# The last batch's inverse transform inside the feed-forward: eight units on four 64x64 tiles in place of sixteen pieces on the full array

## The chip, the cores and the metric

One core of a Trainium2 chip runs the kernel. Its engines are TensorE (PE, with its weight loads as PEld), VectorE (DVE), ScalarE (ACT), GpSimd (POOL) and SyncE (SP), which here issues nearly all DMAs. The metric is device time in microseconds (us) of one execution, as the median of several; less is better.

## The reference

```python
X = np.fft.rfft(x, axis=1)                 # x: 8 batches, 3008 positions, 256 channels
Yr = Xr @ w_r - Xi @ w_i + b_r             # complex linear layer on every frequency
Yi = Xr @ w_i + Xi @ w_r + b_i
Y = softshrink(Yr, 0.01) + 1j * softshrink(Yi, 0.01)
y = np.fft.irfft(Y, n=3008, axis=1)        # 8 x 3008 = 24064 rows of 256
g = y @ w_gate                             # 256 -> 1536
out = (g * sigmoid(g) * (y @ w_val)) @ w_out   # 1536 -> 256
```

## The kernel before

The kernel has two phases. `transform` makes the Fourier transform, the complex layer, the shrink and the inverse transform batch by batch; `gated_ffn` makes the gated feed-forward over 24 blocks of rows. They overlap little: the feed-forward begins at about 520 us and runs to the end.

The second half of the inverse transform (47 positions n for each of 64 residues) is a set of small products. For a residue m and its partner m+32 (index g = 0 or 1) it multiplies, over 48 rows (24 frequencies, real and imaginary), z (48 x 256 channels) with a constant table (48 x 47). For batches 0 to 6 this is done in `transform` by `unit` (lines 616 to 666): a unit takes four m, and as the two g lie at partitions 0 and 64 and the 256 channels are cut in four groups of 64, every matmul uses one 64x64 quarter of the array, 48 rows by 64 columns, with 47 columns moving. It is 4 m x 2 halves of the channels x 2 g x 2 sides = 32 matmuls (line 638), into two PSUM banks, one for each g. ACT copies both banks into an SBUF tile `xt` (line 650, 128x376 each), and a DMA writes it to `xt_d`.

The last batch's rows are needed only by the blocks from 20 on, so its share is done inside the feed-forward by `inverse` (lines 1012 to 1025): 16 pieces of two m, each piece four matmuls of 96 rows (both g in the rows, `co` being a table with zeros between) by 128 columns with 94 columns moving, into the bank `b1`. fp32 matmuls show as two records each, so a piece is 8 records and a unit is 64. ACT copies the bank (line 1024, 128x376), and a DMA writes it out.

In the feed-forward a block has 6 steps q, each with a gate half (n = 0) and a value half (n = 1), made by `gate_or_value` (line 902). Its operations are written out by hand in issue order for PE, DVE, ACT and POOL (`manual_schedule`, line 1052); SP's order is made by the framework. A half makes seven products `up` of three matmuls each (line 780, 128x128 weights, 512 columns; the last two blocks have 384) and, between them, the `down` products of the pair before, of three matmuls each. The matrices are multiplied by a scheme with seven products instead of eight, so sums of inputs and outputs are taken on DVE and POOL. The banks are `b1`, `b2`, `b3`, `spare` and four totals: all eight of PSUM.

The order on PE in the gate half is up 1, up 5, down 1, up 6, down 3, up 2, up 7, up 3, down 2, up 4; the next half begins with up 1 into `b1` and up 5 into `b2`. Where a piece is due (q = 2 of blocks 1 to 16) it stands between up 7 and up 3. `b1` is then free as soon as `take(H11, b1)` has read it, an ACT Silu (line 925) that waits for up 2. After up 3, ACT makes the Silu of H22 (its input is in SBUF) and then of H12 (from `b2`), a cast for T4 (line 796), and after up 4 the Silu of H21. ACT then copies `b1` to `b3` at the start of the next half (line 932).

`load_z` fetches a piece's z and its table (lines 1009, 1010); it is queued in the block before the piece's q = 2. The up weights `wup` come over a ring of four tiles, each loaded three halves ahead (line 215), on the same SP queue.

Of the kernel before, what the change touches and what calls it, by code (L numbers as in the profile page):

```python
# [9 lines left out]
F32 = mybir.dt.float32  # L10
# [7 lines left out]
P = 128  # L18
B = 8
SEQ = 3008  # L20
C = 256
FF = 1536
N1 = 47
N2 = 64
NM = 32
NK = 24
# [3 lines left out]
UM = 4  # L30
NU = NM // UM
UT = UM * 2 * N1
# [33 lines left out]
def fourier_constants():  # L66
    n = float(SEQ)
    k1 = np.arange(NK)
    n1 = np.arange(N1)
    n2 = np.arange(N2)  # L70
    k2 = np.arange(N2)

    def turn(num, den):
        a = 2.0 * np.pi * (np.asarray(num) % den) / den
        c, s = np.cos(a), np.sin(a)
        c[np.abs(c) < 1e-14] = 0.0
        s[np.abs(s) < 1e-14] = 0.0
        return c, s

    c, s = turn(np.outer(n1, k1), N1)  # L80
    wa = np.zeros((2, 64, 2, 32))
    wa[:, :N1, 0, :NK] = c
    wa[:, :N1, 1, :NK] = -s
    wa = wa.reshape(P, 64)

    k = k1[:, None] + N1 * k2[None, :]
    c, s = turn(n2[None, :, None] * k[:, None, :], SEQ)
    re = np.concatenate([c, s], 1)
    im = np.concatenate([-s, c], 1)
    lo = np.arange(N2) < 32  # L90
    wf = np.concatenate([np.where(lo, re, im), np.where(lo, im, re)], 2)
    wf = wf.reshape(NK, 2, 2, 32, P).transpose(2, 1, 3, 0, 4).reshape(P, NK, P)

    c, s = turn(np.outer(k2, n2), N2)
    yr = np.concatenate([c, s], 1)
    yi = np.concatenate([-s, c], 1)
    w = np.where(k2 < 32, 2.0, np.where(k2 == 32, 1.0, 0.0))
    w[0] = 1.0
    wi = []
    for scale in (w, np.full(N2, 2.0)):  # L100
        a, b = yr * scale[:, None], yi * scale[:, None]
        if scale is w:
            b[0] = 0.0
            b[32] = 0.0
        wi.append(np.concatenate([np.where(lo[:, None], a, b), np.where(lo[:, None], b, a)], 0))
    wi = np.stack(wi, 1)

    m = np.arange(NM)
    wo = np.zeros((2, 2, NK, NM, 2, N1))
    for gg in range(2):  # L110
        num = k1[:, None, None] * (64 * n1[None, None, :] + 32 * gg + m[None, :, None])
        c, s = turn(num, SEQ)
        wo[0, gg, :, :, gg] = c / n
        wo[1, gg, 1:, :, gg] = -s[1:] / n
    wq = np.zeros((2, 64, NM * N1))
    for gg in range(2):
        wq[gg, : 2 * NK] = wo[:, gg, :, :, gg].transpose(1, 0, 2, 3).reshape(2 * NK, NM * N1)
    wq = wq.reshape(P, NM * N1)
    wo = wo.reshape(4, NK, NM * 94).transpose(1, 0, 2).reshape(96, NM * 94)
    f = lambda a: np.ascontiguousarray(a, np.float32)  # L120
    return {"wa": f(wa), "wf": f(wf), "wi": f(wi), "wo": f(wo), "wq": f(wq)}


def f32(ap):
# [123 lines left out]


@with_exitstack  # L250
def spectral_ffn(ctx: ExitStack, tc: tile.TileContext, xp, w_r, w_i, cb, wup_raw, wdn_raw, ca, cf, ci, co, cq, out):
    nc = tc.nc
    const = ctx.enter_context(tc.tile_pool(name="const", bufs=1))
    dram = ctx.enter_context(tc.tile_pool(name="dram", bufs=2, space=DRAM))
    w21 = const.tile([P, 2, P], F32R, name="w21")
    ring = ctx.enter_context(tc.tile_pool(name="ring", bufs=RING, reuse_waits="tile"))
    xt_d = [dram.tile([P, 2, SEQ], F32, name=f"xt_d{b}", bufs=1) for b in range(B)]
    d2 = {B - 1: dram.tile([NK, P, C], F32, name="d2_last", bufs=1)}
    wup_d = [dram.tile([P, 2, 7 * P], F32, name=f"wup_d{u}", bufs=1) for u in range(2 * NQ)]
    wdn_d = [dram.tile([P, 2, 7 * P], F32, name=f"wdn_d{q}", bufs=1) for q in range(NQ)]  # L260


    front = ctx.enter_context(tc.tile_pool(name="front", bufs=1))
    ps_ = ctx.enter_context(tc.tile_pool(name="ps", bufs=1, space=PSUM))
    feed = Feed(nc, front, ring, wup_d, xt_d)

    with ExitStack() as tail:
        last = tail.enter_context(tc.tile_pool(name="last", bufs=2, side="right"))
        with ExitStack() as one:
            finish = transform(one, tc, front, ring, last, ps_, feed, xp, w_r, w_i, cb, wup_raw, wdn_raw, ca, cf, ci, cq, w21, wup_d, wdn_d, xt_d, d2)  # L270
        finish()
        ffn = gated_ffn(ctx, tc, front, ring, ps_, feed, co, w21, wdn_d, xt_d, d2[B - 1], out)
        next(ffn)
    next(ffn, None)

# [480 lines left out]
    return finish  # L756


def gated_ffn(ctx, tc, front, ring, ps_, feed, co, w21, wdn_d, xt_d, d2, out):

    nc = tc.nc
    v, g, act = nc.vector, nc.gpsimd, nc.scalar
# [10 lines left out]
    b1, b2, b3, spare = [room(tag) for tag in ("ps_a", "ps_b", "mixb0", "ps_s")]  # L773
# [3 lines left out]
    def product(o, weights, parts, start, stop):  # L777

        for i, (w, x) in enumerate(((1, 0), (0, 0), (0, 1))):
            nc.tensor.matmul(o, lhsT=weights[w], rhs=parts[x], start=start and i == 0, stop=stop and i == 2, skip_group_check=True)  # L780


    H11, H12, H22, H21, T1, T3, T2, T4 = range(8)
    RIGHT = {1: H11, 3: H22, 2: H21, 5: T1, 7: T3, 4: T4, 6: T2}

    def at(i, h):
        return hidden[:, i, :h] if i < 4 else more[:, i - 4, :h]

    def diff(pair, o, a, b):
        h = pair["h"]  # L790
        v.tensor_tensor(at(o, h), at(a, h), at(b, h), op=ALU.subtract)  # L791

    def upper(pair, i):
        h = pair["h"]
        pair[i] = sbr.tile([P, 2, T], F32R, name="h_parts", bufs=8)
        act.copy(pair[i][:, 0, :h], at(i, h))  # L796
# [5 lines left out]
    def down(pair, n_):  # L802

        h, q = pair["h"], pair["q"]
        weights = [wdn[q][:, x, A_AT[n_], :] for x in range(2)]
        parts = [pair[RIGHT[n_]][:, x, :h] for x in range(2)]
        if n_ in total:
            product(total[n_][:, :h], weights, parts, q == 0, q == NQ - 1)
        else:
            product(spare[:, :h], weights, parts, n_ == 1, True)  # L810
# [4 lines left out]
    def add(pair, n_):  # L815
        h = pair["h"]
        o = sums[:, SUM_AT[n_], :h]
        if pair["q"] == 0:
            v.tensor_copy(o, spare[:, :h])
        else:  # L820
            v.tensor_tensor(o, o, spare[:, :h], op=ALU.add)  # L821
# [80 lines left out]
    def gate_or_value(pair, last, n, k, extra):  # L902

        blk, q, h = pair["blk"], pair["q"], pair["h"]
# [17 lines left out]
        def take(i, src):  # L922

            if n == 0:
                act.activation(at(i, h), src, AF.Silu)  # L925
            else:
                v.tensor_tensor(at(i, h), at(i, h), src, op=ALU.mult)  # L927

        gate = n == 0 and last
# [45 lines left out]
        last_sum = b1[:, :h] if n else m5  # L975
        v.tensor_tensor(last_sum, m5, b3[:, :h], op=ALU.add)  # L976
        if gate:
            diff(last, T4, H21, T2)
            add(last, 1)
            if q == 2 and blk in pieces:  # L980
                inverse(pieces[blk])
        up(b2, 3, False)
        take(H22, last_sum)
        take(H12, b2[:, :h])
        if n:
            upper(pair, H22)
            lower(g, pair, H22)
        if gate:
            upper(last, T4)
            lower(g, last, T4)  # L990
            if first:
                step("after d7")
            down(last, 2)
            if closing:
                ends["now"] = result(last)
                step("after d2")
# [3 lines left out]
        take(H21, b3[:, :h])  # L1000


    pieces = {i + 1: i for i in range(NM // 2)}
    part = {}

    def load_z(u):
        z = part["z"] = sbr.tile([96, 2 * C], F32, name="z2")
        w = part["w"] = sbr.tile([96, 2 * 94 + 160], F32, name="w2")[:, : 2 * 94]
        nc.sync.dma_start(z, d2.rearrange("k (q m) c -> (k q) (m c)", m=NM)[:, u * 2 * C : (u + 1) * 2 * C])
        nc.sync.dma_start(w, co[:, u * 188 : (u + 1) * 188])  # L1010

    def inverse(u):
        for cc in range(2):
            for i in range(2):
                nc.tensor.matmul(  # L1015
                    b1[:, cc * 188 + i * 94 : cc * 188 + (i + 1) * 94],
                    lhsT=part["z"][:, i * C + cc * P : i * C + (cc + 1) * P],
                    rhs=part["w"][:, i * 94 : (i + 1) * 94],
                    start=cc == 0 and i == 0,
                    stop=True,  # L1020
                    skip_group_check=True,
                )
        xt = sbr.tile([P, 2, 188], F32, name="xt2")
        act.copy(xt.rearrange("p a b -> p (a b)"), b1[:, :376])
        nc.sync.dma_start(xt_d[B - 1][:, :, u * 188 : (u + 1) * 188], xt)


    todo = {}

# [19 lines left out]
    sbr = ctx.enter_context(tc.tile_pool(name="sb3", bufs=1, side="right", reuse_waits="tile"))  # L1049
    last = None  # L1050
    k = 0
# [57 lines left out]
```

## Time and profile before

| | us |
|---|---|
| median of 3 runs | 2579.42 (2577.97 to 2581.5) |
| the profiled execution | 2577.29 |
| its span, first to last instruction | 2575.3 |
| busy in the span: PE / PEld | 2556.2 / 2141.6 |
| busy: DVE / ACT / POOL | 2060.2 / 1706.7 / 2072.8 |
| granted TensorE clock, mean | 1.000 |

The profiled execution has 2.0 us outside its span. Matmuls overlap each other in the records: a product of three is shown as 0.84 us long, but products follow each other start to start in 0.68 us, and it is starts that are compared below.

### The profile page before, as it was taken

To read this page: it belongs to the slowest core of one execution; us is meant where nothing else is said; L and a number is where in the kernel's file an instruction comes from. 1 tells how busy PE (TensorE), PEld (TensorE's weight loads), DVE (VectorE), ACT (ScalarE), POOL (GpSimd) and SP (SyncE) were. 2 spreads that over 40 slices of the span, in tenths; PEclk is the share of its full clock that TensorE was granted. 3 is DMA by queue.
4 is the path that set the end of the run, shared out by engine and by line. 5 is a ranking of instruction groups with operands and counts; after the bars stand their busy time and mean duration, and the time that the engine had idled before them with its cause. 6 is when DMAs were issued, how large, how long until landed. Compare 5 with 4: busy or idle time off the path is not lost.

```text
span 2575.3 us, 45125 instructions
## 1 busy us (share of the span) xinstructions
PE 2556.2 (99%) x16168; PEld 2141.6 (83%) x16168; DVE 2060.2 (80%) x3001; ACT 1706.7 (66%) x3345; POOL 2072.8 (80%) x1588
## 2 busy tenths in 40 slices
PE   9999999999999999999999999999999999999999
PEld 6788888988888888888888888888888888888899
DVE  7888888668778877877788787878877887888787
ACT  5788888866656666666656666665666666666665
POOL 4777777568888888888888888888888888888886
PEclk9999999999999999999999999999999999999999
DMA  6688888855445444544444455444444444444453
GB/s 231 217 281 275 280 280 264 279 204 190 150 145 167 161 153 153 168 149 146 163 164 151 147 169 168 150 147 159 167 149 144 161 162 149 141 162 158 147 186 122
DMA packets 137360, 460.89 MB, mean 179 GB/s; under 512 B 13872, under 2 KB 61616, under 8 KB 137136
## 3 DMA queue, kind: packets, MB, share of 16 engines
q1 hardware_dynamic: 137136, 458.01, 53.5%
q8 instruction: 128, 2.10, 0.3%
q14 instruction: 96, 0.79, 0.1%
HBM read 366.99 MB, written 90.96 MB: 178 GB/s over the span
## 4 chain that ended last, share of the span: by engine, by line
PE 91%; ACT 4%; DVE 3%; issue 1%; POOL 1%; DMA 1%; ACTq 0%; SPq 0%; POOLq 0%; DVEq 0%
PE bank L780 78%; PE mixb L528 3%; PE ps_b L506 2%; PE ps_s L513 2%; PE ps_z L552 2%; PE ps_a L469 1%; PE ps_x L638 1%; ACT t L540 1%; PE bank L1015 1%; DVE d L474 1%; ACT f_hi L563 0%; ACT z L586 0%; DVE f_lo L566 0%; POOL t L574 0%; DVE f L565 0%
## 5 line engine op out<-in xcount | busy, mean ns | idle before, releaser
L780 PE MATMUL bank<-x_near,wup 128*128 128x512 f32 (+1 forms) x4032 | 1037.5, 386 | 0.3 <-DVE bank L954 0.2
L800 POOL TENSOR_TENSOR h_parts<-more,h_parts 128x512 fp32r<-128x512 f32 (+1 forms) x572 | 847.4, 1494 | 110.5 <-ACT h_parts L796 96.7
L780 PEld LDWEIGHTS bank<-x_near,wup 128*128 128x128 f32 x4032 | 750.6, 188 | 150.9 <-DVE bank L954 3.6
L780 PE MATMUL bank<-h_parts,wdn 128*128 128x512 f32 (+1 forms) x3021 | 835.8, 385 | 0.4 <-DVE h_parts L800 0.4
L800 POOL TENSOR_TENSOR h_parts<-hidden,h_parts 128x512 fp32r<-128x512 f32 (+1 forms) x431 | 563.8, 1319 | 205.4 <-ACT h_parts L796 162.7
L780 PEld LDWEIGHTS bank<-h_parts,wdn 128*128 128x128 f32 x3021 | 564.7, 188 | 109.3 <-DVE h_parts L800 0.7
L796 ACT CAST h_parts<-hidden 128x512 fp32r<-128x512 f32 (+1 forms) x433 | 265.6, 614 | 450.3 <-DVE hidden L927 449.1
L780 PE MATMUL bank<-x_parts,wup 128*128 128x512 f32 (+1 forms) x2016 | 526.5, 384 | 0.0
L927 DVE TENSOR_TENSOR hidden<-hidden,bank 128x512 f32<-128x512 f32 (+1 forms) x576 | 376.0, 674 | 77.9 <-PE bank L780 69.6
L821 DVE TENSOR_TENSOR sums<-sums,bank 128x512 f32<-128x512 f32 (+1 forms) x357 | 240.3, 673 | 243.5 <-PE bank L780 243.4
L780 PEld LDWEIGHTS bank<-x_parts,wup 128*128 128x128 f32 x2016 | 375.2, 188 | 71.3 <-DVE bank L954 1.7
L796 ACT CAST h_parts<-more 128x512 fp32r<-128x512 f32 (+1 forms) x572 | 349.3, 611 | 39.1 <-DVE more L791 28.6
L925 ACT ACTIVATE hidden<-bank 128x512 f32<-128x512 f32 (+1 forms) x432 | 252.6, 585 | 114.7 <-PE bank L780 114.3
L791 DVE TENSOR_TENSOR more<-hidden 128x512 f32<-128x512 f32 (+1 forms) x286 | 291.8, 1059 | 0.0
L791 DVE TENSOR_TENSOR more<-hidden,more 128x512 f32<-128x512 f32 (+1 forms) x286 | 257.6, 901 | 0.0
L932 ACT COPY bank<-bank 128x512 f32<-128x512 f32 (+1 forms) x288 | 161.6, 561 | 109.9 <-DVE hidden L927 103.9
L954 DVE TENSOR_TENSOR bank<-hidden,bank 128x512 f32<-128x512 f32 (+1 forms) x288 | 197.0, 684 | 35.7 <-PE bank L780 23.3
L574 POOL TENSOR_TENSOR t<-t,y 128x512 f32<-128x512 f32 x96 | 132.6, 1382 | 90.3 <-DVE y L573 86.6
L940 ACT COPY hidden<-bank 128x512 f32<-128x512 f32 (+1 forms) x288 | 167.6, 582 | 2.5
L540 ACT COPY t<-mixb 64x256 f32<-64x256 f32 x384 | 140.9, 367 | 21.1 <-PE mixb L528 13.6
L244 POOL TENSOR_TENSOR x_near<-xf,x_near 128x512 fp32r<-128x512 f32 (+1 forms) x112 | 142.1, 1285 | 5.3 <-PE bank L780 4.7
L976 DVE TENSOR_TENSOR hidden<-hidden,bank 128x512 f32<-128x512 f32 (+1 forms) x144 | 97.4, 676 | 43.4 <-PE bank L780 43.2
(107 smaller groups left out, 3105.9 us busy)
## 6 DMA issues: line engine op xcount, KB each, us to landing
wup<-wup_d SPq DMA_DIRECT2D x288, 896.0 KB, 4.6
scratch<-xp SPq DMA_DIRECT2D x59, 512.0 KB, 5.2
out<-o SPq DMA_DIRECT2D x88, 256.0 KB, 6.1
d<-z SPq DMA_DIRECT2D x84, 256.0 KB, 3.9
z_in<-d SPq DMA_DIRECT2D x112, 192.0 KB, 5.0
xt_d<-xt SPq DMA_DIRECT2D x56, 376.0 KB, 5.2
xf<-xt_d SPq DMA_DIRECT2D x15, 1024.0 KB, 6.9
wup_d<-wup SPq DMA_DIRECT2D x12, 896.0 KB, 5.1
```

What stands on the lines that cost most here:

```text
L244: low = lambda: eng.tensor_tensor(part[:, 1, :h], src, f32(part[:, 0, :h]), op=ALU.subtract)
L540: nc.scalar.copy(t()[64 * half : 64 * half + 64, k * C : (k + 1) * C], mixb[64 * k : 64 * k + 64, half * C : (half + 1) * C])
L780: nc.tensor.matmul(o, lhsT=weights[w], rhs=parts[x], start=start and i == 0, stop=stop and i == 2, skip_group_check=True)
L791: v.tensor_tensor(at(o, h), at(a, h), at(b, h), op=ALU.subtract)
L796: act.copy(pair[i][:, 0, :h], at(i, h))
L800: eng.tensor_tensor(pair[i][:, 1, :h], at(i, h), f32(pair[i][:, 0, :h]), op=ALU.subtract)
L821: v.tensor_tensor(o, o, spare[:, :h], op=ALU.add)
L925: act.activation(at(i, h), src, AF.Silu)
L927: v.tensor_tensor(at(i, h), at(i, h), src, op=ALU.mult)
L932: act.copy(b3[:, :h], b1[:, :h])
L940: act.copy(m5, b2[:, :h])
L954: v.tensor_tensor(b2[:, :h], m5, b3[:, :h], op=ALU.add)
```

## The change

The last batch's inverse is made in 8 units of four m, in blocks 1 to 8, in the form that `unit` has: 32 matmuls on four 64x64 tiles, into `b1` for g = 0 and `b2` for g = 1. As `b2` is in use until the Silu of H12 has read it, the unit is issued later, between down 2 and up 4, and in these halves ACT takes H12 ahead of H22. ACT copies `b1` and then `b2` into the z tile itself (its matmuls are done by then), and one DMA of 376 KB writes it out. z is loaded by two DMAs of 192 KB, the table by one from `cq`, which `transform` uses too; the array `co` is gone.

```diff
         if gate:
             diff(last, T4, H21, T2)
             add(last, 1)
-            if q == 2 and blk in pieces:
-                inverse(pieces[blk])
         up(b2, 3, False)
-        take(H22, last_sum)
-        take(H12, b2[:, :h])
+        between = gate and q == 2 and blk in pieces
+        for one in ((H12, b2[:, :h]), (H22, last_sum))[:: 1 if between else -1]:
+            take(*one)
...
             down(last, 2)
+            if between:
+                inverse(pieces[blk])
...
-    pieces = {i + 1: i for i in range(NM // 2)}
+    pieces = {i + 1: i for i in range(NU)}
...
     def load_z(u):
-        z = part["z"] = sbr.tile([96, 2 * C], F32, name="z2")
-        w = part["w"] = sbr.tile([96, 2 * 94 + 160], F32, name="w2")[:, : 2 * 94]
...
+        z = part["z"] = sbr.tile([P, UM * C], F32, name="z2")
+        w = part["w"] = sbr.tile([P, UM * N1], F32, name="w2")
+        rows = d2.rearrange("k (i g m) c -> g (k i) (m c)", i=2, g=2)
+        for g in range(2):
+            nc.sync.dma_start(z[64 * g : 64 * g + 2 * NK], rows[g, :, u * UM * C : (u + 1) * UM * C])
+        nc.sync.dma_start(w, cq[:, u * UM * N1 : (u + 1) * UM * N1])
 
     def inverse(u):
-        for cc in range(2):
-            for i in range(2):
-                nc.tensor.matmul(
-                    b1[:, cc * 188 + i * 94 : cc * 188 + (i + 1) * 94],
...
-        xt = sbr.tile([P, 2, 188], F32, name="xt2")
-        act.copy(xt.rearrange("p a b -> p (a b)"), b1[:, :376])
-        nc.sync.dma_start(xt_d[B - 1][:, :, u * 188 : (u + 1) * 188], xt)
+        for i in range(UM):
+            for cc in range(2):
+                for g, bank in enumerate((b1, b2)):
+                    rows = slice(64 * g, 64 * g + 2 * NK)
+                    for side in range(2):
+                        col = i * C + cc * P + 64 * side
+                        nc.tensor.matmul(
+                            bank[64 * side : 64 * side + 64, (cc * UM + i) * N1 : (cc * UM + i + 1) * N1],
+                            lhsT=part["z"][rows, col : col + 64],
+                            rhs=part["w"][rows, i * N1 : (i + 1) * N1],
...
+        xt = part["z"][:, : 2 * UT].rearrange("p (c t) -> p c t", c=2)
+        to = xt.rearrange("p c (m g n) -> p c m g n", m=UM, g=2)
+        for g, bank in enumerate((b1, b2)):
+            act.copy(to[:, :, :, g], bank[:, : 2 * UM * N1].rearrange("p (c m n) -> p c m n", c=2, m=UM))
+        nc.sync.dma_start(xt_d[B - 1][:, :, u * UT : (u + 1) * UT], xt)
```

## Rows read from the trace of the kernel before

**Rows 1.** The page: busy time of the engines with their share of the span, and the chain of work that ended last, by engine.
```profile
PE 2556.2 (99%) x16168; PEld 2141.6 (83%) x16168; DVE 2060.2 (80%) x3001; ACT 1706.7 (66%) x3345; POOL 2072.8 (80%) x1588
...
PE 91%; ACT 4%; DVE 3%; issue 1%; POOL 1%; DMA 1%; ACTq 0%; SPq 0%; POOLq 0%; DVEq 0%
```

**Rows 2.** The chain that ended last, within 2000 to 2100 us (start us, us, what).
```profile
1999.80 100.39 PE bank L780 x442
```

**Rows 3.** Busy time by stretch: block 16, the last with a piece, block 17, the first without, and block 9, with a piece. The stretch begins and ends at the block's first copy of line 932; columns: us, then PE, PEld, DVE, ACT, POOL busy with counts, granted clock, DMA share, GB/s.
```profile
1917.20:2004.24 87.04, 86.97 (x388) 71.68 (x387) 69.12 (x96) 54.52 (x98) 73.52 (x54) 1.00 0.46 154
2004.24:2090.02 85.78, 85.78 (x380) 70.89 (x379) 69.16 (x96) 53.96 (x97) 73.53 (x54) 1.00 0.46 154
1307.85:1394.88 87.03, 86.96 (x388) 71.70 (x387) 69.22 (x96) 54.59 (x99) 73.56 (x54) 1.00 0.47 157
```

**Rows 4.** The timeline of PE, and one row of PEld, around the piece in block 16: up 2, up 7, the piece, up 3, down 2, up 4 (start us, us, what, count, and in brackets the idle time before and what ended it).
```profile
1948.30 0.84 PE L780 MATMUL bank<-x_near,wup 128*128 128x512 f32 x3
1948.97 0.84 PE L780 MATMUL bank<-x_parts,wup 128*128 128x512 f32 x3
1949.88 1.13 PE L1015 MATMUL bank<-w,z 96*128 96x94 f32 x8
1950.80 0.93 PE L780 MATMUL bank<-x_parts,wup 128*128 128x512 f32 x3
1951.57 0.86 PE L780 MATMUL bank<-h_parts,wdn 128*128 128x512 f32 x3
1952.26 0.85 PE L780 MATMUL bank<-x_parts,wup 128*128 128x512 f32 x3
...
1949.88 0.97 PEld L1015 LDWEIGHTS bank<-w,z 96*128 96x128 f32 x8 [0.49 <-ACT hidden L925]
```

**Rows 5.** The timeline of ACT in the same place: the Silu of H11, the cast for T2, the piece's copy.
```profile
1949.23 0.60 ACT L925 ACTIVATE hidden<-bank 128x512 f32<-128x512 f32 x1 [0.82 <-PE bank L780]
1949.73 0.61 ACT L796 CAST h_parts<-more 128x512 fp32r<-128x512 f32 x1
1951.05 0.47 ACT L1024 COPY xt<-bank 128x376 f32<-128x376 f32 x1 [0.71 <-PE bank L1015]
```

**Rows 6.** The timeline of PE in the same half of block 17, which has no piece: in the first row the last two matmuls of up 2, then up 7 and up 3 (its third matmul is the last of the eight), then down 2, up 4, up 1 of the next half, up 5.
```profile
2035.55 1.98 PE L780 MATMUL bank<-x_near,wup 128*128 128x512 f32 x8
2037.37 0.84 PE L780 MATMUL bank<-h_parts,wdn 128*128 128x512 f32 x3
2038.05 0.84 PE L780 MATMUL bank<-x_near,wup 128*128 128x512 f32 x3
2038.73 0.84 PE L780 MATMUL bank<-x_parts,wup 128*128 128x512 f32 x3
2039.41 0.84 PE L780 MATMUL bank<-x_near,wup 128*128 128x512 f32 x3
```

**Rows 7.** The timeline of ACT in that half: the cast for T2, Silu of H22, Silu of H12, the cast for T4, Silu of H21, the copy of `b1` to `b3`; and DVE's difference that feeds T4.
```profile
2036.76 0.61 ACT L796 CAST h_parts<-more 128x512 fp32r<-128x512 f32 x1
2037.67 0.63 ACT L925 ACTIVATE hidden<-hidden 128x512 f32<-128x512 f32 x1 [0.29 <-POOL h_parts L800]
2038.21 0.58 ACT L925 ACTIVATE hidden<-bank 128x512 f32<-128x512 f32 x1
2038.69 0.61 ACT L796 CAST h_parts<-more 128x512 fp32r<-128x512 f32 x1
2039.19 0.60 ACT L925 ACTIVATE hidden<-bank 128x512 f32<-128x512 f32 x1
2039.83 0.57 ACT L932 COPY bank<-bank 128x512 f32<-128x512 f32 x1
...
2037.49 0.73 DVE L791 TENSOR_TENSOR more<-hidden,more 128x512 f32<-128x512 f32 x1
```

**Rows 8.** The timeline of PE around a unit of `transform` that stands between full-array work: before it 128x256 matmuls, after it 128x512 ones.
```profile
497.13 0.28 PE L513 MATMUL ps_s<-wm_hi,f_lo 128*128 128x256 f32 x1
497.25 0.28 PE L513 MATMUL ps_s<-wm_lo,f_hi 128*128 128x256 f32 x1
497.46 1.15 PE L638 MATMUL ps_x<-wo,z_in 48*64 48x47 f32 x64
498.54 0.50 PE L552 MATMUL ps_z<-y_hi,wi_hi 128*128 128x512 f32 x1
498.88 0.40 PE L552 MATMUL ps_z<-y_lo,wi_hi 128*128 128x512 f32 x1
499.11 0.39 PE L552 MATMUL ps_z<-y_hi,wi_lo 128*128 128x512 f32 x1
```

**Rows 9.** By line: the unit's matmuls and the ACT copy behind a unit, all of them (duration ns min/median/max, first and last start us).
```profile
L638 PE MATMUL ps_x<-wo,z_in x3584: 202/231/253, 108.8 to 521.8; 48*64 48x47 f32 x200
...
L650 ACT COPY xt<-ps_x x112: 469/481/519, 110.0 to 523.4; 128x376 f32<-128x376 f32 x112
```

**Rows 10.** SP's queue around the piece in block 1 (the next piece's loads, this piece's store, the up weights before and behind), and DMA issues by line (KB each, median us to landing).
```profile
639.40 0.33 SPq L215 DMA_DIRECT2D wup<-wup_d  x1
645.36 0.33 SPq L1009 DMA_DIRECT2D z<-d_last  x1
645.75 0.42 SPq L1010 DMA_DIRECT2D w<-co  x1
646.25 0.57 SPq L1025 DMA_DIRECT2D xt_d<-xt  x1
647.46 14.60 SPq L215 DMA_DIRECT2D wup<-wup_d  x3
...
wup<-wup_d SPq DMA_DIRECT2D x288, 896.0 KB, 4.6
...
xt_d<-xt SPq DMA_DIRECT2D x56, 376.0 KB, 5.2
...
xt_d<-xt SPq DMA_DIRECT2D x16, 188.0 KB, 2.7
```

More of the change, by code (lines that the diff above doesn't have):

```diff
@@ L118, in fourier_constants @@
     wq = wq.reshape(P, NM * N1)
-    wo = wo.reshape(4, NK, NM * 94).transpose(1, 0, 2).reshape(96, NM * 94)
     f = lambda a: np.ascontiguousarray(a, np.float32)
-    return {"wa": f(wa), "wf": f(wf), "wi": f(wi), "wo": f(wo), "wq": f(wq)}
+    return {"wa": f(wa), "wf": f(wf), "wi": f(wi), "wq": f(wq)}
 def f32(ap):
@@ L250, in spectral_ffn @@
 @with_exitstack
-def spectral_ffn(ctx: ExitStack, tc: tile.TileContext, xp, w_r, w_i, cb, wup_raw, wdn_raw, ca, cf, ci, co, cq, out):
+def spectral_ffn(ctx: ExitStack, tc: tile.TileContext, xp, w_r, w_i, cb, wup_raw, wdn_raw, ca, cf, ci, cq, out):
     nc = tc.nc
@@ L271, in spectral_ffn @@
         finish()
-        ffn = gated_ffn(ctx, tc, front, ring, ps_, feed, co, w21, wdn_d, xt_d, d2[B - 1], out)
+        ffn = gated_ffn(ctx, tc, front, ring, ps_, feed, cq, w21, wdn_d, xt_d, d2[B - 1], out)
         next(ffn)
@@ L756, in transform, with gated_ffn @@
     return finish
-def gated_ffn(ctx, tc, front, ring, ps_, feed, co, w21, wdn_d, xt_d, d2, out):
+def gated_ffn(ctx, tc, front, ring, ps_, feed, cq, w21, wdn_d, xt_d, d2, out):
     nc = tc.nc
@@ L1000, in gate_or_value @@
         take(H21, b3[:, :h])
-    pieces = {i + 1: i for i in range(NM // 2)}
+    pieces = {i + 1: i for i in range(NU)}
     part = {}
     def load_z(u):
-        z = part["z"] = sbr.tile([96, 2 * C], F32, name="z2")
-        w = part["w"] = sbr.tile([96, 2 * 94 + 160], F32, name="w2")[:, : 2 * 94]
-        nc.sync.dma_start(z, d2.rearrange("k (q m) c -> (k q) (m c)", m=NM)[:, u * 2 * C : (u + 1) * 2 * C])
-        nc.sync.dma_start(w, co[:, u * 188 : (u + 1) * 188])
-    def inverse(u):
-        for cc in range(2):
-            for i in range(2):
-                nc.tensor.matmul(
-                    b1[:, cc * 188 + i * 94 : cc * 188 + (i + 1) * 94],
[L1017 to L1022, printed above, removed]
-        xt = sbr.tile([P, 2, 188], F32, name="xt2")
-        act.copy(xt.rearrange("p a b -> p (a b)"), b1[:, :376])
-        nc.sync.dma_start(xt_d[B - 1][:, :, u * 188 : (u + 1) * 188], xt)
+        z = part["z"] = sbr.tile([P, UM * C], F32, name="z2")
[4 more added lines that the diff above has]
+        nc.sync.dma_start(w, cq[:, u * UM * N1 : (u + 1) * UM * N1])
@@ new lines, in inverse @@
+    def inverse(u):
+        for i in range(UM):
[8 more added lines that the diff above has]
+                            rhs=part["w"][rows, i * N1 : (i + 1) * N1],
+                            start=True,
+                            stop=True,
+                            skip_group_check=True,
+                        )
+        xt = part["z"][:, : 2 * UT].rearrange("p (c t) -> p c t", c=2)
[3 more added lines that the diff above has]
+        nc.sync.dma_start(xt_d[B - 1][:, :, u * UT : (u + 1) * UT], xt)
@@ L1092 @@
         "ci": k["wi"],
-        "co": k["wo"],
         "cq": k["wq"],
```

## The prediction

> **What bounds the kernel now.** I read the page first, then the chain within one stretch, then the busy time by block, and only then the timeline around one piece. On the page PE is busy for 2556.2 of 2575.3 us, and it is 91% of the chain that ended last [rows 1]. Within the feed-forward the chain has nothing but PE: 100 us without a break by line 780 [rows 2]. So whatever PE is spared there shortens the kernel one for one, and whatever makes PE wait lengthens it; the other engines have 20 to 34% of the span free [rows 1]. The blocks by themselves give the price of a piece: 87.04 and 87.03 us with one, 85.78 without, with PE busy to the last tenth and the granted clock at 1.00 in all three [rows 3]. A piece costs 1.25 us, and sixteen of them 16 x 1.25 = 20.0 us.
>
> The timeline shows what those 1.25 us are [rows 4]. Products follow each other by 0.68 us; from up 7 to the piece it is 0.91, so 0.23 are a wait; the piece lasts 0.92 to the start of up 3; up 3 is followed after 0.77 in place of 0.68, as its weights come in late, which is 0.09; down 2 has 0.01 more. The sum is 1.25. The wait is for ACT's Silu of H11, which must read `b1`: up 2 ends at 1949.14, the Silu begins 0.09 later and lasts 0.60, and PE goes on 0.05 behind its end, though up 7 had only covered until 1949.65 [rows 4, 5].
>
> **The change part by part.** *Removed:* sixteen pieces, 20.0 us. Half of that needs no further argument: blocks 9 to 16 become like block 17, which gives 8 x 1.25 = 10.0 us.
>
> *Added: eight units.* The same 32 matmuls on the same four tiles are in the trace, as `unit` [rows 8, 9]. From the unit's first record to the next full-array matmul it is 498.54 - 497.46 = 1.08 us. Going in, the first tile matmul begins 0.21 after the last 256-column one in place of 0.12: 0.09. Going out, the second product matmul begins 0.34 after the first in place of 0.23: 0.11. A unit that waits for nothing so costs 1.08 + 0.09 + 0.11 = 1.28 us.
>
> It has to wait for the Silu of H12, which reads `b2`, and the cover is again one product of three. Up 3 ends at 2037.53 (2035.55 + 1.98) and the place behind down 2 is at 2038.05 [rows 6]. With H12 first, ACT is free for it (the cast for T2 ends at 2037.37), so it begins at 2037.62, takes 0.58 to 0.60 and lets PE go 0.05 later, at 2038.25 to 2038.27 [rows 5, 7]. That is 0.20 to 0.22 behind the place; the wait takes the place of the 0.09 of going in, since in both cases the weights of the first tile matmul are loaded only then. I take 0.22 + 1.08 + 0.11, and 0.01 for the echo in the next product as behind a piece: 1.42 us. The bounds of one unit are 1.28 (no wait) and, from below, those of the first rival, 2.3.
>
> A rule of the Trainium skill speaks against this. The traced unit has 64 records in 1.15 us, the last of them 0.23 long, so its starts lie 0.92 / 63 = 15 ns apart [rows 8, 9]. The page "TensorE: Matmul & The Clock Gate", section "Wait — 56ns, not 53.3ns?", says that matmul starts never come closer than some 25 ns however few columns there are; an estimate by it makes the unit's starts 63 x 25 ns = 1.58 us long, so 0.66 us more than the row, 5.3 us over eight units. By that the time would be 2576 us. The trace doesn't agree, and its rows are of the very shape that is added.
>
> *ACT's part.* Two copies for each unit by 0.48 us [rows 9] stand for two pieces' copies by 0.47 [rows 5]: no more work, but the copy of `b1` must be done before up 1 of the next half. Count from U, the unit's first matmul (2038.27). The unit ends at U + 1.15. ACT by then has made H12 (to U - 0.05), H22 and the cast for T4, which in the plain half follow each other by 0.5 us each [rows 7], so to about U + 1.0; the difference that the cast reads is done at 2038.22. The piece's copy began 0.04 behind its last matmul (1949.88 + 1.13 to 1951.05) [rows 4, 5], a Silu 0.09 behind [rows 5]. So `b1` is read by U + 1.67 to U + 1.72, and PE may go 0.05 later. PE wants it at U + 1.08 + 0.68 + 0.11 = U + 1.87, behind up 4. It is hidden, by 0.1 to 0.15 us. Without that cover PE would pay each tenth eight times, 0.8 us. The copy of `b2` ends by U + 2.2 and is wanted 0.68 later than `b1`: nothing. Behind the copies on ACT stands the Silu of H21, for which up 4 ends at U + 2.03; in the plain half it too starts 0.3 behind its product's end, and the copy to `b3` behind it is wanted only three products later [rows 6, 7]. Swapping H12 and H22 costs nothing else: both are multiplied in the next half.
>
> *DMAs and SP's queue.* Per unit two z loads, a table load and a store stand for four loads and two stores of two pieces. All of it is on SP, none on PE's path unless the up weights behind it come late. The new wait is this: the z tile is also what the store reads, so the next z load must wait until the store has landed, 2.7 us for 188 KB here and 5.2 for 376 KB in the transform, which bound it [rows 10]. SP was already held by such a load, up to 5.9 us in block 1 (639.40 to 645.36), and the next up weights went at 647.46 all the same, because they waited for PE to free a ring tile [rows 10]. With the store issued at about U + 2.3, the hold ends at U + 5.5 to U + 8, near the time when the next up weights are due (7.1 us behind the one before: 14.60 less 0.33, over two [rows 10]). They are needed three halves later and land in 4.6 us; I take nothing.
>
> *The sum.* 20.0 - 8 x 1.42 = 20.0 - 11.4 = 8.6 us. The profiled execution was 2577.29, so it would be 2568.7. The median shown is 2579.42, 2.1 above; what is compared later is such a median, so I predict 2579.4 - 8.6 = **2570.8 us**. Between the bounds of the waits (0.09 going in; a copy late by 0.1 and the next product with it) the saving is 7.8 to 9.8 us.
>
> **The rivals.**
> First, *ACT holds the unit or the next half longer*. If PE's wait is for H22 as well, it is 0.54 us more (2038.21 - 2037.67 [rows 7]), 4.3 us in all: 2575.1. If up 1 waits for both copies, 2.2 + 0.05 - 1.87 = 0.38 more, 3.0 in all: 2573.8. Both together make a unit cost 2.3 us and leave 1.3 us: 2578.1. For it: ACT runs its queue in order and PE sees it through one count. Against it: PE began the piece 0.05 behind the Silu that it needed, while the cast queued behind that was still running (1949.73 to 1950.34) [rows 4, 5].
>
> Second, *PE issues the unit's records further apart than in the transform*. Each ns more between starts costs 63 ns a unit and 0.5 us in all; from 7 ns more on, 22 in place of 15, the saving falls under 5 us, and with ten more it is 3.3: 2576.1. For it: here the unit stands among 512-column products and not among the transform's short ones. Against it: all 3584 records of the transform, whose longest is 253 ns beside a median of 231 [rows 9]. It is the way in which the skill's rule of the closest starts would show.
>
> Third, on the other side: *SP is held so long that PE waits for up weights*. The place is the z load behind the store. An up load is issued three halves ahead, 3 x 7.1 = 21.4 us, and lands in 4.6, so SP may hold it for 17 us before PE waits [rows 10]. Were the store queued on SP a full half or two before its unit, with the up loads behind it and the landing added, a hold of 20 us would cost PE 3 us at each unit: 8 x 3 - 8.6 = 15 us slower, 2595. It decides from a hold of 18 us on, where 8 x 1.1 eats the saving. For it: SP's order is the framework's, and it did set a load 6 us early. Against it: it would have to set it 18 us early.
>
> Fourth, that the change doesn't do what it says: if the units stayed at sixteen pieces' cost by some wait in `transform` or at the start of the feed-forward, where the z tile of 4 KB now lies otherwise, it would be no change, 2579.
>
> **How the numbers follow.** A measurement can tell about 0.2% from no change, 5.2 us: 2574.3 to 2584.6. The forecast with its bounds has 0.82 and is all on the faster side, 2568 to 2573 with the spread of the medians (2577.97 to 2581.5 before). The first rival has 0.10: 0.06 for the copies alone, which is still faster, 0.04 for the H22 wait or both, the same. The second has 0.02, the fourth 0.02, both the same. The third has 0.04, slower. So faster 0.88, same 0.08, slower 0.04. The range from 2567.5 to 2575.5 holds the forecast and most of the first rival.
>
> **What would show it.** Blocks 9 to 16 at 85.78 us, blocks 1 to 8 at 87.2 (85.78 + 1.42). On PE, 64 records of 48x47 between down 2 and up 4, the first 0.88 to 0.90 behind down 2's start in place of 0.68, ended by a wait for the Silu of line 925, and up 4 1.08 behind the first record. On ACT, the copy of `b1` beginning within 0.1 behind the unit, and up 1 0.79 behind up 4. If up 1 comes later than that, the cover of the first copy was wrong; if blocks 9 to 16 aren't like block 17, or PE idles for a DMA of `wup`, the reasoning on what bounds the kernel was.

## The result: slower by 19 us, with the profile after

The changed kernel takes 2598.91 us (median of 4; 2596.28 to 2601.45) beside 2579.48 for the kernel before: a ratio of 1.0078, interval 1.0066 to 1.0091. The forecast was 2570.8.

The page of the changed kernel shows the same picture as [rows 1], PE busy nearly all the time and on the chain, only longer:

```profile
PE 2579.4 (99%) x16552; PEld 2140.7 (82%) x16552; DVE 2041.6 (79%) x3001; ACT 1705.0 (66%) x3345; POOL 2079.4 (80%) x1588
...
PE 92%; ACT 3%; DVE 2%; DMA 1%; POOL 1%; issue 1%; SPq 0%; ACTq 0%; DVEq 0%; POOLq 0%
```

The stretches of three blocks of the changed kernel answer to [rows 3]: block 17, which never had a piece; block 8, the last with a unit, and block 9, now without.

```profile
2021.43:2108.51 87.08, 87.08 (x380) 70.95 (x379) 68.39 (x96) 53.92 (x98) 73.81 (x54) 1.00 0.45 151
1147.84:1236.31 88.47, 88.47 (x444) 71.94 (x443) 68.35 (x96) 55.04 (x100) 73.68 (x54) 1.00 0.49 159
1324.74:1411.82 87.08, 87.08 (x380) 70.95 (x379) 68.37 (x96) 53.92 (x98) 73.79 (x54) 1.00 0.46 151
```

Block 9 is like block 17, as forecast, and a unit costs 88.47 - 87.08 = 1.39 us where 1.42 was expected. But block 17 is not what it was: 87.08 in place of 85.78. It runs the same 378 matmuls of 512 columns in the same order at the same clock, PE is busy throughout, and each block loses 1.30 us. Over 22 blocks that is 28.6 us, against some 9 gained.

The timeline of PE in block 17 of the changed kernel shows where. Products followed each other by 0.68 us in [rows 6].

```profile
2069.50 0.87 PE L779 MATMUL bank<-h_parts,wdn 128*128 128x512 f32 x3
2070.20 0.85 PE L779 MATMUL bank<-x_near,wup 128*128 128x512 f32 x3
2070.89 0.84 PE L779 MATMUL bank<-x_parts,wup 128*128 128x512 f32 x3
2071.57 0.84 PE L779 MATMUL bank<-x_near,wup 128*128 128x512 f32 x3
2072.25 0.86 PE L779 MATMUL bank<-h_parts,wdn 128*128 128x512 f32 x3
2072.95 0.85 PE L779 MATMUL bank<-x_near,wup 128*128 128x512 f32 x3
```

A down product (`h_parts,wdn`) now takes 0.70 to the next start, the product right behind it 0.69, and the ones behind that 0.68 as ever. The groups by shape in that stretch say the same; first of the changed kernel, then of the kernel before in its block 17 (mean ns after the count and busy time):

```profile
L779 PE MATMUL bank<-x_near,wup 128*128 128x512 f32 x221 | 59.2, 391 | 0.0
L779 PE MATMUL bank<-h_parts,wdn 128*128 128x512 f32 x126 | 36.3, 396 | 0.0
L779 PE MATMUL bank<-x_parts,wup 128*128 128x512 f32 x33 | 9.3, 389 | 0.0
```

```profile
L780 PE MATMUL bank<-x_near,wup 128*128 128x512 f32 x221 | 58.9, 389 | 0.0
L780 PE MATMUL bank<-h_parts,wdn 128*128 128x512 f32 x126 | 35.4, 389 | 0.0
L780 PE MATMUL bank<-x_parts,wup 128*128 128x512 f32 x33 | 9.3, 389 | 0.0
```

No idle time stands in any row: nothing waits, the matmuls with `h_parts` as moving operand are themselves slower, by 7 ns of 389. So the loss is neither in the unit nor behind a wait. The one difference found for `h_parts` in a block without a unit is where it lies. It comes from the pool `sb3`, which grows down from the top of SBUF and also holds the tiles of the inverse. These were 4944 bytes a partition and are 4848 now: the z tile grew by 2048 bytes, the table tile shrank by 640 with its `+ 160` gone, and the store's own tile of 1504 went. The addresses in the two built programs:

```
            before                     changed
h_parts     191616 = 128 x 1497        191712 = 128 x 1497 + 96
z2          224384 = 128 x 1753        224480 = 128 x 1753 + 96
x_near       46208 = 128 x  361         46208
wup          17536 = 128 x  137         17536
wdn0        107648 = 128 x  841        107648
```

### The profile page after: what moved, and what is told of

The parts are those of the page before. It is cut to its first block, busy times and chain, and to the rows that moved or that the text cites. A ratio compares the mean times of both kernels' runs of the same rounds, so it can differ in the third digit from the quotient of the medians.

```text
span 2599.5 us, 45892 instructions
## 1 busy us (share of the span) xinstructions
PE 2579.4 (99%) x16552; PEld 2140.7 (82%) x16552; DVE 2041.6 (79%) x3001; ACT 1705.0 (66%) x3345; POOL 2079.4 (80%) x1588
## 4 chain that ended last, share of the span: by engine, by line
PE 92%; ACT 3%; DVE 2%; DMA 1%; POOL 1%; issue 1%; SPq 0%; ACTq 0%; DVEq 0%; POOLq 0%
PE bank L779 79%; PE mixb L527 4%; PE ps_b L505 2%; PE ps_s L512 2%; PE ps_z L551 2%; PE ps_a L468 1%; PE ps_x L637 1%; ACT t L539 1%; ACT z L585 0%; ACT f_hi L562 0%; DMA xf<-xt_d 0%; POOL t L573 0%; DVE f_lo L565 0%; PE bank L1021 0%; DVE f L564 0%
## 5 line engine op out<-in xcount | busy, mean ns | idle before, releaser
L779 PE MATMUL bank<-h_parts,wdn 128*128 128x512 f32 (+1 forms) x3021 | 856.7, 392 | 0.3 <-DVE h_parts L799 0.3
L790 DVE TENSOR_TENSOR more<-hidden 128x512 f32<-128x512 f32 (+1 forms) x286 | 282.9, 1027 | 0.0
L790 DVE TENSOR_TENSOR more<-hidden,more 128x512 f32<-128x512 f32 (+1 forms) x286 | 246.3, 861 | 0.0
```

## The experiments

The first theory was that the address of the moving operand sets the speed of the down products; the rival was something that the unit leaves behind. All medians below are device time; the times of the kernel before beside them were 2577.5 to 2578.5. "Offset" is the distance of an address above a multiple of 128 bytes.

| kernel | offset of | median, us | a plain block, us |
|---|---|---|---|
| before | none | 2579.5 | 85.78 |
| changed | h_parts 96 | 2598.9 | 87.08 |
| pad_128 | none | 2568.3 | 85.76 |
| pad_64 | h_parts 64 | 2608.9 | 87.64 |
| before_off32 (with the 16 pieces) | h_parts 32 | 2616.1 | 87.52 |
| view_16 | h_parts 16 | 2599.1 | 87.15 |
| view_4 | h_parts 4 | 2629.8 | 88.57 |
| xparts_64 | x_parts 64 | 2591.1 | 86.54 |
| wdn_64 | down weights 64 | 2586.6 | 86.55 |
| wup_64 | up weights 64 | 2610.1 | 87.62 |
| h_wdn_64 | h_parts and down weights 64 | 2603.9 | 87.40 |
| weights_64 | both weights 64 | 2609.8 | 87.54 |
| all_64 | all of these 64 | 2568.4 | 85.79 |

The plain block is block 17 in each profile; in xparts_64 only 12 of its 126 products read x_parts.

One thing about the edits matters for the reading. In wdn_64, h_wdn_64, wup_64, weights_64, view_16 and view_4 the edited tiles are also 128 bytes longer, so that each next one lies 128 bytes further on. Their offset to a multiple of 128 is the one in the table for all of them, but to a multiple of 256 it alternates, by 128. In the built programs every operand of the up and down products of the 24 blocks lies 128 past a multiple of 256 in the kernel before and in pad_128, and 192 past one in all_64.

**pad_64.** Only the table tile is longer:

```diff
-        w = part["w"] = sbr.tile([P, UM * N1], F32, name="w2")
+        w = part["w"] = sbr.tile([P, UM * N1 + 12], F32, name="w2")[:, : UM * N1]
```

> The changed kernel with the unit's table tile 12 floats longer and nothing else. The eight h_parts tiles, which lie below it on the same side, move down by 32 bytes: from 32 past a multiple of 64 bytes (191712) to a multiple (191680). Theory, the address of the down products' moving operand: blocks 9 to 21 go back from 87.08 to 85.78 us, blocks 1 to 8 from 88.43 to 87.13, and the median is 2599 less 29 (22 blocks by 1.30, the two short ones 0.4), so 2570, inside 2568 to 2573. Rival, something that the unit's form leaves behind (the order of DMAs on SP, the reuse of the z tile, the Silu order): nothing moves, 2599.

It took 2608.86 us (ratio to the kernel before 1.0117, 1.0101 to 1.0133), slower than the changed kernel by 10. Neither theory holds as put: the address matters, as twelve unused floats slow every block, but a multiple of 64 is no cure. Block 17:

```profile
2026.64:2114.28 87.64, 87.64 (x380) 70.97 (x379) 68.13 (x96) 54.07 (x97) 73.75 (x54) 1.00 0.44 150
```

**before_off32.** The kernel before, its table tile 8 floats shorter:

```diff
-        w = part["w"] = sbr.tile([96, 2 * 94 + 160], F32, name="w2")[:, : 2 * 94]
+        w = part["w"] = sbr.tile([96, 2 * 94 + 152], F32, name="w2")[:, : 2 * 94]
```

> The kernel before with its table tile 8 floats shorter (1360 bytes in place of 1392) and nothing else, so that h_parts lies at 191648, 32 past a multiple of 64 bytes. No unit, no new order. Theory of the address: plain blocks at 87.08 us in place of 85.78, the median at 2579.5 + 29 = 2608. Rival, the unit's form: nothing moves, 2579.5.

2616.12 us (1.0145, 1.0129 to 1.0161), in the direction of the address theory and 8 us beyond its number. The unit and the new order have no part in the loss, since they aren't in this kernel. Block 17:

```profile
2033.38:2120.90 87.52, 87.52 (x380) 70.96 (x379) 68.08 (x96) 53.97 (x97) 73.81 (x54) 1.00 0.45 151
```

**pad_128.** As pad_64 with `+ 28` in place of `+ 12`.

> As pad_64 but with 28 floats more, so that h_parts lies at 191616, a multiple of 128 bytes as in the kernel before, where pad_64 has an odd multiple of 64. If 64 bytes are what counts: the same as pad_64 within 0.1%, 2570. If 128 bytes count: pad_64 keeps a part of the loss (half of 29 would be 2585) and only this one is at 2570.

2568.26 us, a ratio of 0.9959 (0.9945 to 0.9974) to the kernel before: with `h_parts` back at its old address the loss is gone, and this version beats both kernels. That 128 bytes are the unit doesn't follow, as it is the same address. It is the change as it was meant, with the loss taken away: 2598.91 - 2568.26 = 30.7 us is the price of the address (29.5 with each kernel set against the times of the kernel before that were taken beside it). Blocks 17, 7 and 9 of pad_128:

```profile
1995.16:2080.92 85.76, 85.76 (x380) 70.89 (x379) 69.14 (x96) 53.94 (x98) 73.55 (x54) 1.00 0.45 154
1134.82:1221.95 87.13, 87.13 (x444) 71.87 (x443) 69.11 (x96) 55.06 (x99) 73.48 (x54) 1.00 0.49 161
1309.09:1394.84 85.75, 85.75 (x380) 70.86 (x379) 69.10 (x96) 53.91 (x97) 73.53 (x54) 1.00 0.46 154
```

The next four, all from pad_128 or pad_64, ask which operand's address, how fine, and against what it is measured.

**xparts_64.**

```diff
-    sums = sb.tile([P, 3, T], F32, name="sums")
+    sums = sb.tile([P, 3 * T + 16], F32, name="sums")[:, : 3 * T].rearrange("p (a b) -> p a b", b=T)
```

> Base is pad_128 (2568.3 us). The tile `sums` is 16 floats longer, so that x_parts (and the output tiles o) lie 64 past a multiple of 128 bytes; h_parts stays on a multiple. x_parts is the moving operand of 2016 of the 6048 up matmuls, 672 products. Theory, any moving operand off a multiple of 128 bytes slows its product, by what pad_64 showed for h_parts (1.88 us over 42 products of a block, 0.045 us each): 672 x 0.045 = 30 us, 2598, and products on x_near stay as they are in blocks where no x_parts stands before them. Rival, something peculiar to h_parts (its writers on ACT and POOL, its place beside the unit's tiles): 2568.

2591.12 us, 23 lost where 30 were expected: nothing is peculiar to `h_parts`. The loss grows with the products that a block makes on x_parts: in the trace block 19, which has none, takes 85.70 us, block 17 with 12 takes 86.54, and block 18 with 48 takes 87.37.

**wdn_64.** The down weights are read from 16 floats into longer tiles:

```diff
-        wdn.append(down_pool.tile([P, 2, 7, P], F32R, name=f"wdn{len(wdn)}"))
+        wdn.append(down_pool.tile([P, 14 * P + 32], F32R, name=f"wdn{len(wdn)}")[:, 16 : 16 + 14 * P].rearrange("p (i n a) -> p i n a", i=2, n=7))
```

> Base is pad_128 (2568.3 us). The six tiles of the down weights are read at 64 past a multiple of 128 bytes, all else stays on multiples. Theory, only the moving operand counts: 2568. Rival, each operand that PE reads counts: the same 42 products of a block are slowed, by about as much as in pad_64, 2608.

2586.57 us: 18 lost. The theory of the moving operand alone falls, as weights count too, though by less than the rival's 40.

The trace shows more. A step q multiplies the down weights of the step before, each step from its own tile. Steps 2 to 5 of block 17, from up 1 to up 1, come out alternately short and long; in pad_128 each takes 14.28 us, shown first for its step 2:

```profile
2022.82:2037.10 14.28, 14.28 (x64) 11.83 (x63) 10.92 (x16) 8.37 (x16) 12.43 (x10) 1.00 0.38 134
```

```profile
2038.64:2052.97 14.33, 14.33 (x64) 11.83 (x63) 10.73 (x16) 8.35 (x16) 12.34 (x10) 1.00 0.37 130
2052.97:2067.48 14.51, 14.51 (x64) 11.82 (x63) 10.77 (x16) 9.44 (x18) 12.50 (x10) 1.00 0.38 127
2067.48:2081.81 14.33, 14.33 (x65) 11.83 (x63) 10.73 (x16) 9.38 (x18) 12.25 (x10) 1.00 0.37 130
2081.81:2096.32 14.51, 14.51 (x64) 11.83 (x63) 10.78 (x16) 9.94 (x19) 12.99 (x11) 1.00 0.38 128
```

The weights of these steps lie 320, 448, 64 and 192 bytes past a multiple of 512, the `h_parts` 128 past one. So 64 and 320 cost the same 0.05 us, 192 and 448 the same 0.23: a move by 256 bytes changes nothing, a move by 128 does. What counts here is the offset to a multiple of 256, and the 18 us are the mean of a cheap and a dear position.

**view_16.** As pad_128, with

```diff
-        pair[i] = sbr.tile([P, 2, T], F32R, name="h_parts", bufs=8)
+        pair[i] = sbr.tile([P, 2 * T + 32], F32R, name="h_parts", bufs=8)[:, 4 : 4 + 2 * T].rearrange("p (a b) -> p a b", b=T)
```

> Base is pad_128 (2568.3 us). The h_parts tiles begin on multiples of 128 bytes but are written and read from 16 bytes in. If it is the line of 128 bytes that a row of 512 floats straddles: a loss of the size of the other offsets (32: 38 us, 64: 41, 96: 31), so 2595 to 2610. If only the granule of 32 bytes in which these offsets differ counts, none: 2568.

2599.08 us: 31 lost, so no granule of 32 bytes saves it. Like that of wdn_64 the loss mixes two positions, since every other tile lies 128 bytes further on.

**all_64.** pad_64 with 16 floats more behind the first tile of SBUF, which moves up every tile on the left side:

```diff
-    w21 = const.tile([P, 2, P], F32R, name="w21")
+    w21 = const.tile([P, 2 * P + 16], F32R, name="w21")[:, : 2 * P].rearrange("p (a b) -> p a b", b=P)
```

> pad_64 (2608.9 us) with every other tile of SBUF from the up weights to the outputs moved up by 64 bytes as well, so that moving operands and weights have the same distance to a multiple of 128 bytes. If what counts is the distance between the weights and the moving operand, or between one moving operand and the next: no loss, 2568. If it is the address of the moving operand by itself: the up products lose too, 126 products of a block in place of 42 by 0.045 us, so 22 x 5.6 + two short blocks = 125 to 130 us above 2568, near 2695.

2568.35 us. This is the run that turned the explanation: `h_parts` lies exactly where it lay in pad_64 (2608.86), and the 40 us are gone, because weights and x moved with it. So this address is not bad by itself; what counts is how it lies to the others. Its block 17, beside pad_64's above:

```profile
1995.07:2080.86 85.79, 85.79 (x380) 70.89 (x379) 69.20 (x96) 53.96 (x98) 73.55 (x54) 1.00 0.45 154
```

Two theories were left: the *pair* (a moving operand and the weights loaded beside it) and the *switch* (a change of offset from one moving operand, or one set of weights, to the next).

**h_wdn_64.** pad_64 with the edit of wdn_64.

> pad_64 (h_parts 64 past a multiple of 128 bytes, 2608.9 us) with the down weights also 64 past. Two theories are left after all_64. Theory of the pair: what costs is a moving operand and the weights that are loaded beside it (those of the next matmul) at different distances to a multiple of 128 bytes. Then the two inner pairs of a down product agree again, only the first and the last pair at its borders differ, and less is lost than in pad_64: 2585 to 2600. Theory of the switch: each change of the distance from one moving operand to the next, and from one set of weights to the next, costs. Then the losses add, 41 of pad_64 and 18 of wdn_64: 2625.

2603.85 us, above the pair's range by 4 and below the switch's number by 21. The losses don't add, and agreeing inside the down product helps little: 36 are lost in place of 41. Nor is it that `h_parts` and weights agree to a multiple of 128 only: in three of the six steps they agree to a multiple of 256 as well, and in block 17 these still lose 0.26 us each to pad_128, the others 0.27, and pad_64's 0.31.

**wup_64.** pad_128 with the ring tile of `feed.unit` read 16 floats in, as the down weights in wdn_64.

> pad_128 (2568.3 us) with only the up weights 64 past a multiple of 128 bytes. Up products are 84 of a block's 126, and most stand in runs without a down product. Theory of the pair: every up matmul whose successor is an up matmul runs beside weights at another distance, so the loss is there all along, also in the runs of up products, 84 x 0.02 to 0.045 us a block, 2603 to 2650. Theory of the switch: inside a run of up products the starts stay 227 ns apart and only the borders to down products cost, as many as in wdn_64: about 2586.

2610.05 us, inside the pair's range, and the loss stands inside the runs of up products too. In the timeline of PE in its block 17, the nine matmuls of three up products in a row take 2029.92 - 2027.85 = 2.07 us start to start where 9 x 0.227 = 2.04 were due, and single up products 0.69 to 0.70:

```profile
2027.85 2.23 PE L779 MATMUL bank<-x_near,wup 128*128 128x512 f32 x9
2029.92 0.86 PE L779 MATMUL bank<-h_parts,wdn 128*128 128x512 f32 x3
2030.62 0.86 PE L779 MATMUL bank<-x_near,wup 128*128 128x512 f32 x3
2031.31 0.86 PE L779 MATMUL bank<-x_parts,wup 128*128 128x512 f32 x3
2032.01 0.86 PE L779 MATMUL bank<-x_near,wup 128*128 128x512 f32 x3
2032.71 0.85 PE L779 MATMUL bank<-h_parts,wdn 128*128 128x512 f32 x3
```

That is what the pair theory asked for and not the switch, but there are borders to down products all around. weights_64 takes them away.

**weights_64.** The edits of wdn_64 and wup_64 together.

> pad_128 (2568.3 us) with the up and the down weights both 64 past a multiple of 128 bytes and all moving operands on multiples. The distance never changes from one moving operand to the next, nor from one set of weights to the next, but every matmul runs beside weights at another distance. Theory of the pair: each of a block's 378 matmuls starts 6 to 7 ns later, as in the long runs of up products in wup_64 (233 to 234 in place of 227), 2.5 us a block and 22 blocks, 2568 + 56 = 2624. Theory of the switch: no loss, 2568.

2609.77 us: 41.5 lost. The tiles of both weights alternate between 64 and 192 past a multiple of 256, with all moving operands 128 past one. In the gate half of step 2 up and down weights are both at 64, in that of step 3 both at 192, so no offset changes there from product to product. Up 1, up 5, down 1, up 6, down 3 and the next products in these two halves of block 17:

```profile
2055.76 0.85 PE L779 MATMUL bank<-x_parts,wup 128*128 128x512 f32 x3
2056.44 0.85 PE L779 MATMUL bank<-x_near,wup 128*128 128x512 f32 x3
2057.13 0.85 PE L779 MATMUL bank<-h_parts,wdn 128*128 128x512 f32 x3
2057.82 0.85 PE L779 MATMUL bank<-x_near,wup 128*128 128x512 f32 x3
2058.50 0.85 PE L779 MATMUL bank<-h_parts,wdn 128*128 128x512 f32 x3
2059.19 2.22 PE L779 MATMUL bank<-x_near,wup 128*128 128x512 f32 x9
```

```profile
2070.30 0.86 PE L779 MATMUL bank<-x_parts,wup 128*128 128x512 f32 x3
2070.99 0.86 PE L779 MATMUL bank<-x_near,wup 128*128 128x512 f32 x3
2071.70 0.86 PE L779 MATMUL bank<-h_parts,wdn 128*128 128x512 f32 x3
2072.39 0.86 PE L779 MATMUL bank<-x_near,wup 128*128 128x512 f32 x3
2073.10 0.86 PE L779 MATMUL bank<-h_parts,wdn 128*128 128x512 f32 x3
```

The five products take 3.43 us in the first and, with the next at 2073.80, 3.50 in the second, where 3.40 were due: every product is late, though nothing switches, so the switch theory falls. The size is less than the pair theory said (56): (87.54 - 85.76) / 378 = 4.7 ns a matmul, not 6 to 7. Nor does the loss count pairs: wup_64, in which a third of the matmuls read weights that had not moved, lost as much.

**view_4.** As view_16, with `1 : 1 + 2 * T`.

> Base is pad_128 (2568.3 us), with h_parts written and read from 4 bytes in, the smallest shift of a float. By view_16 (2599) the straddling of a line of 128 bytes is enough: 2590 to 2600. If a finer granule counts, of 16 bytes or more: 2568.

2629.76 us, 61 lost: no granule of 16 bytes either, and twice the loss of view_16. But not all of it is the matmuls' own pace. In block 17 of view_4, unlike the others, the weights also wait, six times, for ACT's copy of `b1` to `b3` (idle us in total, times, longest):

```profile
PEld bank L779 <- ACT bank L931: 1.7, 6, 0.4
```

So its number isn't to be set beside the other offsets'.

## Why the prediction was wrong

*What bounds the kernel: right.* PE is on the chain throughout, and what was added to its matmuls came through one for one: 1.30 us in each of 22 blocks, less some 9 gained, is the 19 by which the kernel is slower.

*The saving: right.* pad_128 has the change without the loss and saves 10.1 us by the medians of its own comparison (2578.33 to 2568.26; 7 to 14 by the interval), where 8.6 were forecast and 20.0 - 8 x 1.37 = 9.0 follow from the blocks. Blocks 9 to 16 became like block 17. A unit costs 87.13 - 85.76 = 1.37 us in place of 1.42, but its parts were not those forecast. PE around the unit in block 7 of pad_128:

```profile
1167.92 0.84 PE L779 MATMUL bank<-h_parts,wdn 128*128 128x512 f32 x3
1168.69 1.21 PE L1021 MATMUL bank<-w,z 48*64 48x47 f32 x64
1169.84 2.34 PE L779 MATMUL bank<-x_near,wup 128*128 128x512 f32 x9
1172.02 0.84 PE L779 MATMUL bank<-h_parts,wdn 128*128 128x512 f32 x3
```

and ACT there, the Silu of H12, of H22, the cast for T4, the two copies:

```profile
1168.12 0.60 ACT L924 ACTIVATE hidden<-bank 128x512 f32<-128x512 f32 x1 [0.20 <-PE bank L779]
1168.62 0.62 ACT L924 ACTIVATE hidden<-hidden 128x512 f32<-128x512 f32 x1
1169.13 0.61 ACT L795 CAST h_parts<-more 128x512 fp32r<-128x512 f32 x1
1169.87 0.99 ACT L1032 COPY z<-bank 128x376 f32<-128x376 f32 x2
```

The unit begins 0.77 behind down 2, not 0.88 to 0.90: at 1168.69, before the Silu of H12 ends at 1168.72. Its first matmuls write `b1`, which had long been free, and only those into `b2` need that Silu. So 0.09 of going in is left, and the rest of the wait is inside the unit, which lasts 1.15 to up 4 in place of 1.08. Going out is 0.14 in place of 0.11 plus 0.01 (2.18 us from up 4 to the next down product, 9 x 0.227 = 2.04). The sum, 0.09 + 1.15 + 0.14 = 1.38, is the block's 1.37 within the rounding. That the forecast 1.42 came so near is in part luck: the wait came out at 0.16 (0.09, and 0.07 inside the unit) in place of 0.22, the way out at 0.14 in place of 0.12.

*ACT's part: right.* The copies begin as the unit ends and are over at 1170.86; up 1, the fourth matmul behind 1169.84, isn't late, since all nine matmuls lose only the 0.14 of going out.

*SP's queue: nothing, as taken.* The trace of the changed kernel has no wait of PE or of its weight loads for a DMA of `wup`; the third rival fell, and with it its price of 15 us. That the kernel came out slower all the same isn't to its credit.

*The first and second rival fell too.* PE waited neither for H22 nor for both copies. The 64 records of the unit take 1.21 us beside 1.15 in the transform, with a part of the wait inside; the second rival's 7 ns more between starts would have added 0.44.

*The step that failed* is the base of the sum. "Blocks 9 to 16 become like block 17" was right, but block 17 stood at 85.78 us as something that the edit could not touch, so what the new tiles do to the blocks without a unit was put at nothing, without a reason. Measured, it became 87.08. Only the fourth rival saw that "the z tile of 4 KB now lies otherwise", and it looked for a wait that would at most undo the saving. The diff has the cause: the z tile grows, the table tile loses `+ 160`, and three tiles of `sb3` become two. No instruction on `h_parts` is touched, but its address moves by 96 bytes, and 42 of a block's 126 products read it. That term is 30.7 us, three times the saving, and had no place in the sum nor in the range. pad_128 takes it away with 28 unused floats, and before_off32 brings a like loss into the kernel before with none of the change, so that the cause is shown.

## What to carry to other kernels

Read a diff for tile sizes as well as for instructions: a tile that grows, shrinks or goes moves all that is allocated beyond it in the same pool, and an odd pad can be a sign that an address is being kept; taking 8 floats from the one here cost 38 us (before_off32). Where PE is the bound, compare the offsets of moving operands and weights to a multiple of 256 bytes before and after; here one of them moved against the others by 16 to 96 bytes cost 0.7 to 1.6% of the time. When a trace shows the same instructions with no idle time, each a few ns longer, compare addresses before looking for waits: a pad of a few floats is the test. And when a tile is padded, look where the pad puts its neighbours.

## What the runs showed of the hardware

PE's matmuls of 512 columns start 227 ns apart when all that PE reads has the same offset to a multiple of 256 bytes, whether that is 128 (the kernel before, pad_128) or 192 (all_64). When weights and moving operands differ by 64 they start later: by 4.7 ns on average with all weights off (weights_64). There a product of three matmuls is 6 to 7 ns late in the gate half of step 2, where the weights lie 64 below the moving operand, and 17 to 22 in that of step 3, where they lie 64 above. A move by 256 changes nothing (wdn_64). A difference of 128 alone was not tried, nor was a uniform shift other than 64.

The lateness doesn't stay with the matmuls that differ. In the changed kernel (`h_parts` off by 96) a down product is 24 ns late, the up product behind it 9, and the others not at all. In pad_64 (off by 64) nearly all are late, and the up products, whose own operands agree, have more than half of the loss: up 1, two products behind a down one, 11 ns, and up 5 behind it 17. These are the same nanoseconds in every block, and in the gate half and the value half, in which ACT, DVE and POOL do different work. So nothing points to a collision with those engines, but no run was made to exclude it.

The Trainium skill's page "SBUF — State Buffer", section "Who interferes with whom", gives PE two read ports, one for the moving operand and one for weights, as independent, and says that PE never waits on anyone. By this the place of the weights should cost nothing, and the runs here don't agree: moving the weights by 64 bytes against the moving operands cost 41.5 us (weights_64).

Open is what lies under it. That the offset of weights and moving operands to each other counts is shown; which reads meet, those of one matmul or of neighbours, and how, is not: with agreeing offsets inside the down product (h_wdn_64) 36 us of 41 were still lost. The losses for `h_parts` at 32, 64 and 96 bytes are 38 (against the kernel before), 41 and 31 us, without an order that I can name.

One thing more. In view_4, where `h_parts` is written from 4 bytes in, POOL's subtractions into it are shown shorter, not longer, 1209 ns beside 1521 in pad_128 (block 17 of each, first of view_4):

```profile
L799 POOL TENSOR_TENSOR h_parts<-more,h_parts 128x512 fp32r<-128x512 f32 x24 | 29.0, 1209 | 14.3 <-ACT h_parts L795 14.2
...
L790 DVE TENSOR_TENSOR more<-hidden,more 128x512 f32<-128x512 f32 x12 | 14.1, 1179 | 0.0
```

```profile
L799 POOL TENSOR_TENSOR h_parts<-more,h_parts 128x512 fp32r<-128x512 f32 x24 | 36.2, 1521 | 3.8 <-ACT h_parts L795 3.8
...
L790 DVE TENSOR_TENSOR more<-hidden,more 128x512 f32<-128x512 f32 x12 | 10.9, 911 | 0.0
```

DVE's differences beside them are longer by 268 ns, so the two may have changed places in something that they share; spans on POOL are rough, and no run was made to tell.
